# Attention, Fourier mixing and a feed-forward on one core: sums of four split over two engines, folds taken crosswise, special columns in two column groups

## The chip, the core and the metric

The kernel runs on one core of a Trainium2 chip. The core has TensorE (PE: matmuls, into the eight banks of PSUM), VectorE (DVE), ScalarE (ACT) and GpSimd (POOL) for elementwise work, and SyncE (SP), whose queue issues most DMAs here; GpSimd's queue issues the rest. Every engine works through its own queue in order and waits on semaphores for the others. The metric is the device time of one execution in microseconds, the median of several runs.

## What is computed

Eight batches of eight heads, 576 positions, head size 64. Attention is the sum of two parts: one over means of four neighbouring positions, repeated four times, and one over positions less than four apart. Its output goes through a two-dimensional Fourier transform, of which the real part is added, then a layer norm and a feed-forward with a width of 2048.

```python
q_d = q.reshape(B, H, Sd, factor, D).mean(axis=3)     # factor 4, Sd = 144; k_d, v_d alike
out_up = np.repeat(sm_attn(q_d, k_d, v_d), factor, axis=2)
mask = np.abs(pos[:, None] - pos[None, :]) < factor
...                                                   # softmax of the masked scores
x = out_up + out_local                                # as (B, S, H * D)
mixed = np.real(np.fft.fft(np.fft.fft(x, axis=1), axis=2))
u = x + mixed
un = (u - mu) / np.sqrt(var + 1e-06)
return u + np.maximum(un @ w_ch1, 0.0) @ w_ch2
```

## The kernel before

There are three kinds of work, and they overlap. `Unit` (40 of them, five for each batch) loads a span of 128 positions of queries and keys (`qkT`, six buffers) and of values (`vaug`), sums queries and keys in fours (`sum_in`, L603, into `sums`), computes the local attention of two windows of 64 positions and writes it to `xa` (front half of the positions) and `xb` (the back half, in reversed order). `Pooled` (one for each batch) computes the attention over the sums of four: `scores` (L473) need `sums` of all five units of the batch; `pool_v` (L447) sums the values by matmuls in groups of 32 array columns; the result goes to `odt`, and `pack` sends a last piece by DMA into slot 2 of `xa`.

`Mix` (one for each batch) is the Fourier transform, as matmuls with cosine and sine tables. Since cosine is even and sine odd, the work is halved by folding the positions (front with back) and the channels (1 to 255 with 511 to 257) before the matmuls. `half_sum` (L744, VectorE) and `half_difference` (L747, GpSimd) fold positions, 512 columns each for each of three slots, into `xs` and `xm` (`halves`); `channels` (L755, VectorE) folds channels, 255 columns with the second input reversed; `fold` (L768, VectorE for the sum and GpSimd for the difference) folds once more into `f`; `sequence` (L793) is the matmul over positions, `mix` (L832, L828) the one over channels, `unfold` (L851) undoes the folds, and the stores go to DRAM. Channels 0 and 256 have no partner. `split_z` (L781, ScalarE) copies them into `zs`, padded with zeros to 66 columns; `sequence_z` (L808) multiplies them, eight matmul passes for a batch (four slots, two passes each in float32); `z_high` and `z_low` (L811, L814) copy rows 0 to 3 of the result and its rounding rest to rows 0 to 3 and 32 to 35 of `yz`, which `clear_yz` has zeroed; `mix` adds them with the rows of `signs`.

`Quarter` decodes the weights (64 pieces; ScalarE, GpSimd, three VectorE operations, ScalarE, GpSimd). `Block` (nine, of 512 tokens) is norm and feed-forward: `first` (L1172) and `second` (L1192 to L1194) are its matmuls in the first three blocks; the later six use a product with fewer multiplications (L1110), for which `Differences` prepares differences of weights.

The order is written out by hand. `at(fn)` gives each call a place from `TURNS`, in the order of the calls of its kind; calls without a place come after all others, by a time `t` that the planner counts. All calls are then made in the order of places, and each engine's queue and each DMA queue is filled in that order. There are 1574 places: the attention, the mixing, the weights, block 0 and part of block 1 have them. No call can overtake another on its engine. PSUM banks are handed out in that order too.

Of the kernel before, what the change touches and what calls it, by code (L numbers as in the profile page):

```python
# [8 lines left out]
F32 = mybir.dt.float32  # L9
# [4 lines left out]
ALU = mybir.AluOpType  # L14
# [8 lines left out]
ZCOLS = 66  # L23
# [3 lines left out]
    "Pooled.pool_v": (49, 130, 261, 398, 518, 677, 799, 920),  # L27
    "Pooled.copy_v": (50, 132, 263, 399, 520, 680, 800, 925),
# [4 lines left out]
    "Pooled.maxima": (  # L33
        43, 19, 20, 166, 83, 109, 283, 207, 224, 427, 332, 353, 552, 488, 511, 697, 617, 641, 823, 746, 770,
        952, 865, 891,
    ),
    "Pooled.exps": (
        46, 23, 30, 173, 86, 115, 288, 216, 231, 435, 339, 361, 558, 502, 519, 703, 620, 650, 837, 756, 780,
        954, 869, 896,
    ),  # L40
    "Pooled.transpose_p": (
        59, 26, 35, 176, 110, 134, 312, 228, 265, 441, 351, 386, 584, 503, 523, 710, 643, 683, 839, 774, 806,
        958, 894, 926,
    ),
    "Pooled.copy_p": (
        68, 29, 56, 190, 114, 139, 315, 234, 268, 443, 360, 410, 588, 509, 533, 714, 649, 687, 846, 779, 816,
        964, 897, 931,
    ),
    "Pooled.values": (
        88, 51, 62, 198, 133, 142, 320, 264, 277, 445, 400, 413, 602, 522, 537, 727, 684, 698, 852, 803, 821,  # L50
        965, 927, 949,
    ),
    "Pooled.result": (
        93, 54, 71, 202, 155, 154, 323, 273, 284, 454, 408, 416, 605, 542, 544, 730, 694, 701, 856, 809, 826,
        972, 935, 951,
    ),
    "Pooled.store": (97, 212, 392, 463, 626, 750, 878, 975),
    "Pooled.pack": (100, 213, 342, 493, 624, 747, 871, 977),
    "Mix.half_sum": (
        120, 91, 125, 247, 252, 253, 352, 355, 372, 513, 515, 526, 636, 658, 662, 763, 762, 786, 887, 905, 904,  # L60
        1000, 1004, 1003,
    ),
    "Mix.half_difference": (
        112, 95, 111, 219, 255, 280, 356, 379, 380, 504, 529, 531, 646, 663, 665, 767, 795, 794, 885, 918, 915,
        999, 994, 1009,
    ),
    "Mix.channels": (
# [4 lines left out]
    ),  # L72
    "Mix.fold": (
# [4 lines left out]
    ),  # L78
    "Mix.split_z": (84, 137, 191, 287, 362, 382, 535, 534, 681, 686, 777, 836, 930, 921, 983, 1014),
    "Mix.sequence_z": (165, 311, 440, 573, 705, 841, 960, 1016),  # L80
    "Mix.z_high": (175, 316, 457, 587, 715, 847, 1022, 1054),
    "Mix.z_low": (182, 326, 474, 590, 720, 859, 1031, 1064),
    "Mix.sequence": (
        181, 180, 178, 179, 330, 331, 329, 327, 480, 481, 465, 466, 608, 615, 576, 586, 740, 743, 741, 739, 860,
        861, 879, 881, 1010, 1011, 987, 1007, 1071, 1070, 1107, 1102,
    ),
    "Mix.sequence_out": (193, 189, 341, 337, 484, 470, 621, 597, 755, 754, 868, 886, 1021, 1024, 1120, 1111),
    "Mix.mix": (
        239, 266, 227, 260, 350, 368, 385, 387, 366, 418, 497, 521, 500, 536, 642, 654, 631, 685, 676, 678, 772,
        804, 768, 773, 895, 900, 928, 957, 893, 901, 1069, 1072, 1068, 1029, 1131, 1157, 1186, 1214, 1185, 1213,  # L90
    ),
    "Mix.even_out": (
        262, 235, 363, 389, 390, 501, 508, 648, 634, 679, 778, 775, 898, 933, 922, 1079, 1080, 1143, 1208, 1194,
    ),
    "Mix.unfold": (
        281, 286, 270, 271, 375, 374, 404, 403, 425, 426, 539, 543, 549, 551, 660, 659, 702, 695, 689, 690, 814,
        813, 788, 787, 911, 910, 969, 968, 934, 939, 1098, 1134, 1101, 1099, 1178, 1180, 1233, 1232, 1217, 1219,
    ),
    "Mix.store_mixed": (307, 423, 625, 708, 876, 976, 1159, 1235),
    "Mix.store_local": (143, 150, 244, 309, 394, 462, 564, 572, 707, 668, 752, 783, 877, 973, 998, 1006),  # L100
    "Mix.store_ends": (496, 835, 974, 1220),
    "Unit.load": (
        2, 3, 1, 0, 7, 40, 41, 58, 57, 38, 99, 146, 147, 145, 148, 243, 149, 246, 208, 245, 396, 424, 421, 391,
        461, 568, 567, 569, 571, 595, 623, 669, 667, 709, 670, 785, 748, 832, 784, 833,
    ),
    "Unit.sum_in": (
        9, 10, 11, 12, 13, 42, 53, 64, 66, 73, 168, 172, 183, 184, 185, 282, 297, 300, 321, 324, 432, 449, 450,
        475, 477, 579, 583, 591, 593, 607, 688, 696, 733, 734, 735, 829, 830, 853, 855, 857,
    ),
    "Unit.load_v": (  # L110
        8, 36, 37, 39, 4, 5, 102, 98, 101, 103, 211, 242, 144, 209, 241, 308, 345, 393, 395, 346, 397, 490, 492,
        491, 494, 565, 627, 628, 596, 666, 751, 671, 753, 749, 782, 834, 874, 875, 872, 873,
    ),
    "Unit.scores": (
        14, 15, 25, 61, 48, 74, 104, 117, 119, 141, 199, 220, 236, 237, 319, 291, 365, 384, 420, 447, 468, 517,
        545, 585, 601, 610, 629, 652, 699, 725, 726, 781, 802, 820, 825, 864, 899, 943, 940, 956,
    ),
    "Unit.maxima": (
        21, 18, 45, 65, 52, 80, 107, 121, 123, 169, 206, 223, 275, 250, 333, 299, 373, 409, 429, 451, 478, 524,
        553, 592, 603, 618, 635, 656, 700, 731, 736, 790, 808, 824, 828, 866, 908, 953, 944, 967,  # L120
    ),
    "Unit.exps": (
        24, 22, 47, 70, 55, 85, 113, 131, 135, 174, 215, 230, 289, 259, 338, 303, 383, 434, 444, 458, 485, 532,
        559, 599, 619, 622, 647, 672, 704, 737, 738, 801, 815, 838, 844, 870, 923, 955, 948, 978,
    ),
    "Unit.transpose_p": (
        27, 28, 60, 75, 89, 116, 118, 164, 177, 204, 229, 238, 293, 294, 347, 367, 412, 446, 469, 499, 547, 546,
        577, 609, 632, 674, 653, 711, 712, 760, 759, 805, 840, 842, 880, 919, 929, 981, 959, 980,
    ),
    "Unit.copy_p": (  # L130
        31, 32, 67, 78, 94, 129, 138, 188, 195, 214, 233, 258, 304, 305, 358, 388, 436, 456, 472, 506, 557, 556,
        589, 611, 644, 682, 673, 716, 723, 764, 776, 817, 845, 849, 883, 924, 932, 982, 961, 990,
    ),
    "Unit.values": (
# [111 lines left out]
def kernel(  # L246
# [475 lines left out]
    for t in (zs, *(t[:, :, DM:] for t in halves)):  # L722
        nc.gpsimd.memset(t, 0.0)
# [729 lines left out]
```

## Time and profile before

| | us |
|---|---|
| median of 3 runs | 1124.72 |
| lowest and highest run | 1123.99, 1129.9 |
| span of the profiled execution (its first to its last instruction) | 1124.3 |
| TensorE busy in it | 1070.8 |
| VectorE, ScalarE, GpSimd busy | 637.6, 401.0, 352.0 |

The profile is one execution. Busy time is the union of an engine's instructions; matmul passes are pipelined, so many of them overlap, and the mean time of one pass is longer than its share of the busy time. A chain of waits is followed back from the last instruction: at each step to what released it, or to the instruction before it on its engine. "SPq" is time in SyncE's queue, "issue" time in which the engine waited for nothing that the profile shows.

### The profile page before, as it was taken

The numbers are of one execution on the slowest core, as the hardware profiler recorded it, in microseconds if no ns is written. First come the engines' busy times: TensorE is split into PE (matmuls) and PEld (weight loads), VectorE is DVE, ScalarE is ACT, GpSimd is POOL, SyncE is SP. The second block draws the span as 40 slices with busy tenths as digits, with TensorE's granted clock in tenths as the row PEclk, the third lists the DMA queues.
The fourth block names the chain that finished last, engine by engine and source line by source line (L and its number), as shares of the span: only waits on it lengthen the run. The fifth ranks groups of instructions, "written<-read, shape, count | busy, mean of one in ns | idle before, by whom it ended". The sixth has DMA issues, their size and how long they took to land.

```text
span 1124.3 us, 24306 instructions
## 1 busy us (share of the span) xinstructions
PE 1070.8 (95%) x9316; PEld 899.0 (80%) x9316; DVE 637.6 (57%) x1298; ACT 401.0 (36%) x1122; POOL 352.0 (31%) x501
## 2 busy tenths in 40 slices
PE   7787998999999999999999999999999999999998
PEld 5565766777778888887788889888989889889997
DVE  4778889988999885452314533443443343353333
ACT  4756565675444442132221231232232132132121
POOL 1313231233475553487331140331231331222000
PEclk9999999999999999999999999999999999999999
DMA  6545647676685444478709845955955975875641
GB/s 246 187 168 189 223 140 226 226 229 175 181 193 169 123 122 140 111 241 279 194 1 278 245 152 166 314 171 160 298 194 162 259 236 159 221 252 183 216 160 38
DMA packets 121451, 214.36 MB, mean 191 GB/s; under 512 B 14576, under 2 KB 30992, under 8 KB 121208
## 3 DMA queue, kind: packets, MB, share of 16 engines
q1 hardware_dynamic: 110056, 191.97, 52.0%
q0 software_dynamic: 11280, 20.84, 10.2%
q8 instruction: 74, 1.21, 0.4%
q14 instruction: 41, 0.34, 0.1%
HBM read 166.86 MB, written 45.42 MB: 189 GB/s over the span
## 4 chain that ended last, share of the span: by engine, by line
PE 67%; DMA 13%; DVE 9%; SPq 4%; POOL 3%; issue 3%; ACT 2%; DVEq 0%; ACTq 0%; POOLq 0%
PE banks L1110 18%; PE banks L1192 10%; PE banks L1193 10%; PE banks L1194 10%; PE banks L1172 7%; PE banks L793 3%; DMA w1l<-ut 2%; DMA qkT<-in_qk_dram 2%; DMA w1h<-ut 2%; PE banks L832 2%; PE banks L522 1%; DMA raw<-in_wq_dram 1%; DMA vaug<-in_vw_dram 1%; PE banks L1039 1%; DMA out_dram<-ut 1%
## 5 line engine op out<-in xcount | busy, mean ns | idle before, releaser
L1192 PE MATMUL banks<-w2h,hh 128*128 128x512 f32 x576 | 228.4, 397 | 0.7 <-ACT hh L1176 0.7
L1194 PE MATMUL banks<-w2h,hl 128*128 128x512 f32 x576 | 225.0, 391 | 0.8 <-DVE hl L1180 0.8
L1193 PE MATMUL banks<-w2l,hh 128*128 128x512 f32 x576 | 225.4, 391 | 0.0
L1176 ACT ACTIVATE hh<-row 128x512 fp32r<-128x512 f32 x96 | 60.6, 632 | 285.8 <-DVE row L1135 194.2
L1135 DVE TENSOR_TENSOR row<-wt,banks 128x256 f32<-128x256 f32 x192 | 80.4, 419 | 142.9 <-PE banks L1110 138.7
L1180 DVE SCALAR_TENSOR_TENSOR hl<-row,hh 128x512 fp32r<-128x512 f32 x96 | 68.9, 718 | 118.8 <-ACT hh L1176 118.8
L1194 PEld LDWEIGHTS banks<-w2h,hl 128*128 128x128 f32 x576 | 108.2, 188 | 25.5 <-DVE hl L1180 1.7
L1192 PEld LDWEIGHTS banks<-w2h,hh 128*128 128x128 f32 x576 | 108.5, 188 | 20.7 <-ACT hh L1176 1.1
L1193 PEld LDWEIGHTS banks<-w2l,hh 128*128 128x128 f32 x576 | 108.6, 188 | 19.2
L1172 PE MATMUL banks<-unT,w1h 128*128 128x512 f32 x384 | 102.3, 392 | 0.6 <-DVE unT L1048 0.6
L1172 PEld LDWEIGHTS banks<-unT,w1h 128*128 128x128 f32 x384 | 71.7, 188 | 16.4 <-DVE unT L1048 1.0
L1009 POOL DMA_DIRECT2D ut<-ux x40 | 35.7, 1034 | 152.4 <-DMA ut<-um 124.7
L1180 DVE SCALAR_TENSOR_TENSOR hl<-banks,hh 128x512 fp32r<-128x512 f32 x48 | 32.8, 688 | 77.5 <-ACT hh L1176 77.5
L639 ACT ACTIVATE sb<-banks,mx 128x64 f32<-128x64 f32 x320 | 70.0, 330 | 1.3
L1130 ACT COPY wt<-banks 128x256 f32<-128x256 f32 x96 | 35.8, 372 | 95.4 <-PE banks L1110 95.4
L793 PE MATMUL banks<-seq,f 128*128 128x290 f32 x256 | 67.0, 412 | 2.1 <-ACT sb L639 1.4
L1110 PE MATMUL banks<-w1h,w1h 128*128 128x256 f32 x384 | 62.0, 283 | 3.1 <-DMA w1h<-ut 3.0
L1110 PE MATMUL banks<-w1h,w1l 128*128 128x256 f32 x384 | 62.6, 285 | 2.4 <-DMA w1l<-ut 2.0
L1110 PE MATMUL banks<-unT,w1h 128*128 128x256 f32 x432 | 63.4, 283 | 0.0
L1110 PE MATMUL banks<-unT,w1l 128*128 128x256 f32 x432 | 63.2, 282 | 0.0
L1110 PEld LDWEIGHTS banks<-unT,w1h 128*128 128x128 f32 x432 | 59.8, 190 | 3.9
L1110 PEld LDWEIGHTS banks<-unT,w1l 128*128 128x128 f32 x432 | 59.8, 191 | 3.7
(122 smaller groups left out, 1929.1 us busy)
## 6 DMA issues: line engine op xcount, KB each, us to landing
w1l<-ut SPq DMA_DIRECT2D x96, 256.0 KB
w1h<-ut SPq DMA_DIRECT2D x96, 256.0 KB
qkT<-in_qk_dram SPq DMA_DIRECT2D x40, 512.0 KB
w1h<-ub SPq DMA_DIRECT2D x72, 256.0 KB
w1l<-ub SPq DMA_DIRECT2D x72, 256.0 KB
raw<-in_wq_dram SPq DMA_DIRECT2D x64, 256.0 KB
vaug<-in_vw_dram SPq DMA_DIRECT2D x40, 260.0 KB
out_dram<-ut SPq DMA_DIRECT2D x36, 256.0 KB
```

The costliest lines, as they stand in the source:

```text
L639: nc.scalar.activation(out=self.sb[:, hp, z], in_=self.sc[:, z, hp], func=AF.Exp, scale=0.125, bias=self.mx[:, z, hp : hp + 1],)
L793: nc.tensor.matmul(y, l, r, start=(i == 0), stop=(i == len(mms) - 1))
L1009: nc.gpsimd.dma_start(out=to, in_=ux[b][k0 : k0 + m, :], accum_op=ALU.add)
L1110: nc.tensor.matmul(into, w[:, y, c, :], both[z][:, c, :], start=(start and i == 0), stop=(i == len(mms) - 1), skip_group_check=True)
L1130: nc.scalar.copy(out=joins[k].bitcast(F32), in_=self.ps[x])
L1135: nc.vector.tensor_add(out=place(to), in0=place(a), in1=self.ps[x])
L1172: nc.tensor.matmul(hps, a[:, c, :], unT[:, x, c, :], start=(i == 0), stop=(i == len(mms) - 1))
L1176: nc.scalar.activation(out=hh, in_=self.hps[f], func=AF.Relu)
L1180: nc.vector.scalar_tensor_tensor(out=hl, in0=self.hps[f], scalar=0.0, in1=self.hh[f].bitcast(F32), op0=ALU.max, op1=ALU.subtract)
L1192: nc.tensor.matmul(acc, hh, w2h, start=start, stop=False)
L1193: nc.tensor.matmul(acc, hh, w2l, start=False, stop=False)
L1194: nc.tensor.matmul(acc, hl, w2h, start=False, stop=stop)
```

## The change

Three edits of the arithmetic, and new places for all calls.

Sums of four: `pair_in` adds elements 0, 1 to elements 2, 3 of each four on GpSimd (512 columns out, into `half`, two buffers), and `sum_in` adds the two halves on VectorE, in place of one reduction over four.

Crosswise folds: `cross` adds near channels 1 to 255 of one half of the positions to the reversed far channels of the other half, once each way (VectorE for the one, GpSimd for the other, 255 columns each). `channels` then takes sum and difference of the two. `half_sum` and `half_difference` go.

Special columns: `split_z` adds channels 0 and 256 of both halves on GpSimd (three slots) and copies those of the pooled part on ScalarE. `zs` has 32 columns. `sequence_z` sends slots alternately to output rows 0 to 31 and 32 to 63; `z_high` and `z_low` copy all 64 rows; `signs` has ones in each group of 32 and so adds the groups. `clear_yz` goes.

Places: 1937 calls have one now. New are those of the first three blocks to their end, of the start of block 3, and of `Differences`.

```diff
-ZCOLS = 66
+ZCOLS = 32
 TURNS = {
     "Pooled.scores": (
-        33, 17, 16, 163, 77, 105, 276, 200, 221, 419, 328, 348, 548, 483, 498, 675, 614, 633, 818, 744, 758,
-        950, 862, 882,
+        41, 34, 40, 160, 90, 105, 292, 228, 259, 420, 365, 390, 576, 508, 537, 713, 647, 652, 843, 789, 806,
+        962, 914, 924,
     ),
+    "Unit.pair_in": (
+        5, 1, 21, 24, 9, 38, 79, 67, 28, 50, 162, 192, 106, 202, 213, 346, 288, 335, 294, 352, 452, 472, 378,
+        483, 453, 598, 603, 627, 630, 619, 692, 775, 675, 738, 761, 783, 872, 780, 877, 888,
     ),
...
+        def pair_in(self):
+
+            self.half = pd.tile([P, 2 * HP, GU, 2], F32, name="half", bufs=2)
+            x = self.qkT.rearrange("p i h (g r) -> p (i h) g r", r=4)
+            nc.gpsimd.tensor_add(out=self.half, in0=x[:, :, :, 0:2], in1=x[:, :, :, 2:4])
+
         def sum_in(self):
...
-            x = self.qkT.rearrange("p i h (g r) -> p (i h) g r", r=4)
+            x = self.half
             n = sum(g < GH for g in groups_of(self.m))
             for a, e in ((0, n), (n, GU)):
                 if a < e:
                     to = out[:, :, a:e] if e == n else out[:, :, a:e][:, :, ::-1]
-                    nc.vector.tensor_reduce(out=to, in_=x[:, :, a:e], axis=AX.X, op=ALU.add)
+                    nc.vector.tensor_add(out=to, in0=x[:, :, a:e, 0], in1=x[:, :, a:e, 1])
...
-        def half_sum(self, t):
-            nc.vector.tensor_add(out=halves[0][:, t, :DM], in0=xa[:, t], in1=xb[:, t])
-
-        def half_difference(self, t):
-            nc.gpsimd.tensor_sub(out=halves[1][:, t, :DM], in0=xa[:, t], in1=xb[:, t])
+        def cross(self, t, back):
+            near, far = (xb, xa) if back else (xa, xb)
+            (nc.gpsimd if back else nc.vector).tensor_tensor(
+                out=crossed[back][:, t, 1:HD], in0=near[:, t, 1:HD], in1=far[:, t, DM - 1 : HD : -1], op=ALU.add
+            )
...
-            src = odt[:, 0] if t == NSL else halves[odd][:, t]
+            if t == NSL:
+                a, b = odt[:, 0, 1:HD], odt[:, 0, DM - 1 : HD : -1]
+            else:
+                a, b = (x[:, t, 1:HD] for x in crossed)
             nc.vector.tensor_tensor(
-                out=self.w[t][:, odd, 1:HD],
-                in0=src[:, 1:HD],
-                in1=src[:, DM - 1 : HD : -1],
-                op=ALU.subtract if odd else ALU.add,
+                out=self.w[t][:, odd, 1:HD], in0=a, in1=b, op=ALU.subtract if odd else ALU.add
             )
...
         def split_z(self, pooled):
+            cols = slice(0, HD + 1, HD)
             if pooled:
-                z, x = zs[:, NSL:], odt[:, 0:1, 0 : HD + 1 : HD]
+                nc.scalar.copy(out=zs[:, NSL:, 0:2], in_=odt[:, 0:1, cols])
             else:
-                z, x = zs[:, :NSL], halves[0][:, :, 0 : HD + 1 : HD]
-            nc.scalar.copy(out=z[:, :, 0:2], in_=x)
+                nc.gpsimd.tensor_add(out=zs[:, :NSL, 0:2], in0=xa[:, :, cols], in1=xb[:, :, cols])
...
         def sequence_z(self):
 
-            y = self.yzp = bank(self, "yz", ZCOLS)[:, 0, :KEPT]
-            mms = self.slots(zs, 0)
-            for i, (l, r) in enumerate(mms):
-                nc.tensor.matmul(y, l, r, start=(i == 0), stop=(i == len(mms) - 1))
+            y = self.yzp = bank(self, "yz", 2 * ZCOLS)[:, 0, :KEPT]
+            for i, (l, r) in enumerate(self.slots(zs, 0)):
+                g = i % 2 * ZCOLS
+                nc.tensor.matmul(y[g : g + ZCOLS], l, r, start=(i < 2), stop=(i >= 2), skip_group_check=True)
 
         def z_high(self):
-            nc.scalar.copy(out=yz[0:4, self.mine], in_=self.yzp[0:4])
+            nc.scalar.copy(out=yz[: 2 * ZCOLS, self.mine], in_=self.yzp)
 
         def z_low(self):
-            nc.vector.tensor_sub(out=yz[32:36, self.mine], in0=self.yzp[0:4], in1=yz[0:4, self.mine].bitcast(F32))
+            high = yz[: 2 * ZCOLS, self.mine].bitcast(F32)
+            nc.vector.tensor_sub(out=yz[2 * ZCOLS :, self.mine], in0=self.yzp, in1=high)
...
-    signs[[0, 2, 32, 34]] = 1.0
-    signs[[1, 3, 33, 35]] = [1.0, -1.0]
+    signs[0::32] = 1.0
+    signs[1::32] = [1.0, -1.0]
```

## Rows read from the trace of the kernel before

**Rows 1.** The page: busy us (share, instructions) of engines; busy tenths in 40 slices.
```profile
PE 1070.8 (95%) x9316; PEld 899.0 (80%) x9316; DVE 637.6 (57%) x1298; ACT 401.0 (36%) x1122; POOL 352.0 (31%) x501
...
PE   7787998999999999999999999999999999999998
...
DVE  4778889988999885452314533443443343353333
```

**Rows 2.** Three stretches: length, busy us by engine, granted clock, DMA share, GB/s.
```profile
0.00:336.00 336.00, 297.45 (x4930) 222.99 (x4931) 278.04 (x571) 191.17 (x661) 109.31 (x162) 0.98 0.65 199
336.00:588.00 252.00, 250.16 (x1118) 204.91 (x1117) 138.25 (x263) 80.24 (x189) 135.47 (x195) 1.00 0.53 154
588.00:1124.30 536.30, 523.18 (x3271) 471.12 (x3270) 221.31 (x465) 129.61 (x273) 107.27 (x144) 1.00 0.66 202
```

**Rows 3.** The chain of waits, 0 to 340 us: shares by line; start, us, what.
```profile
by line: PE banks L793 10.1%; DMA qkT<-in_qk_dram 6.6%; issue 5.7%; PE banks L522 4.4%; DMA raw<-in_wq_dram 4.4%; DMA vaug<-in_vw_dram 4.3%; PE banks L832 4.0%; DVE sums L603 3.1%; DMA um<-o 2.9%; PE banks L652 2.8%; SPq L884 2.8%; PE banks
...
9.83 4.67 DVE sums L603 x5
...
92.31 1.74 DVE xs L744 x2
```

**Rows 4.** Groups by line and shape: busy us, mean ns of one, idle before.
```profile
L603 DVE TENSOR_REDUCE sums<-qkT 128x256 f32<-128x1024 f32 x32 | 38.4, 1211 | 12.4 <-DMA qkT<-in_qk_dram 8.0 <-PE banks L473 4.3
L747 POOL TENSOR_TENSOR xm<-xa,xb 128x512 f32<-128x512 f32 x24 | 35.4, 1481 | 39.2 <-DMA xa<-rest 19.9 <-DVE xb L700 13.7 <-DMA vaug<-in_vw_dram 5.5
L768 POOL TENSOR_TENSOR f<-w 128x256 f32<-128x256 f32 x32 | 26.6, 845 | 62.0 <-DVE w L755 57.8 <-DVE rsd L534 4.3
L744 DVE TENSOR_TENSOR xs<-xa,xb 128x512 f32<-128x512 f32 x24 | 19.0, 805 | 5.8 <-DMA xa<-rest 5.6
L768 DVE TENSOR_TENSOR f<-w 128x256 f32<-128x256 f32 x32 | 18.1, 571 | 0.1
L808 PE MATMUL banks<-seq,z 128*66 128x290 f32 x64 | 17.1, 410 | 0.4 <-DVE ends L851 0.4
L447 PE MATMUL banks<-vaug,poolm 128*32 128x260 f32 x128 | 11.0, 414 | 5.5 <-DMA vaug<-in_vw_dram 5.3 <-ACT ptd L507 0.2
L603 DVE TENSOR_REDUCE sums<-qkT 128x136 f32<-128x544 f32 x8 | 5.7, 711 | 0.0
L603 DVE TENSOR_REDUCE sums<-qkT 128x120 f32<-128x480 f32 x8 | 5.2, 646 | 0.1
```

**Rows 5.** VectorE in order of time, 87.5 to 100: start, us, line, what.
```profile
87.86 0.69 DVE L744 TENSOR_TENSOR xs<-xa,xb 128x512 f32<-128x512 f32 x1 [2.31 <-DMA xa<-rest]
88.58 1.37 DVE L755 TENSOR_TENSOR w<-xs 128x255 f32<-128x255 f32 x1
...
97.47 0.41 DVE L755 TENSOR_TENSOR w<-xs 128x255 f32<-128x255 f32 x1
...
99.00 1.21 DVE L603 TENSOR_REDUCE sums<-qkT 128x256 f32<-128x1024 f32 x1
```

**Rows 6.** GpSimd in order of time, the same stretch.
```profile
87.99 3.11 POOL L747 TENSOR_TENSOR xm<-xa,xb 128x512 f32<-128x512 f32 x2 [3.69 <-DMA xa<-rest]
...
99.02 1.30 POOL L747 TENSOR_TENSOR xm<-xa,xb 128x512 f32<-128x512 f32 x1
```

**Rows 7.** TensorE in order of time, from 247.8 us.
```profile
247.84 2.12 PE L808 MATMUL banks<-seq,z 128*66 128x290 f32 x8
249.80 0.60 PE L652 MATMUL banks<-ident,sb 128*128 128x128 f32 x4
```

**Rows 8.** TensorE in order of time, from 284.8 us.
```profile
284.77 2.12 PE L808 MATMUL banks<-seq,z 128*66 128x290 f32 x8
286.82 0.73 PE L522 MATMUL banks<-vsum,ptd 128*32 128x65 f32 x32
```

**Rows 9.** Who waited for whom, 0 to 340, TensorE: us, times, longest.
```profile
PE banks L473 <- DVE sums L603: 3.8, 2, 3.6
```

**Rows 10.** Who waited for whom, 0 to 340, GpSimd.
```profile
POOL f L768 <- DVE w L755: 57.8, 14, 10.1
```

More of the change, by code (lines that the diff above doesn't have):

```diff
@@ L66 @@
+        1005, 966, 979,
+    ),
+    "Pooled.store": (
+        97, 234, 344, 513, 674, 765, 958, 989,
+    ),
+    "Pooled.pack": (
+        132, 199, 366, 518, 651, 784, 904, 1016,
+    ),
+    "Mix.cross": (
[3 rows of a table added]
     ),
     "Mix.channels": (
[4 rows of a table removed]
[4 rows of a table added]
     ),
     "Mix.fold": (
[4 rows of a table removed]
-    ),
-    "Mix.split_z": (84, 137, 191, 287, 362, 382, 535, 534, 681, 686, 777, 836, 930, 921, 983, 1014),
-    "Mix.sequence_z": (165, 311, 440, 573, 705, 841, 960, 1016),
-    "Mix.z_high": (175, 316, 457, 587, 715, 847, 1022, 1054),
@@ L82 @@
-    "Mix.z_low": (182, 326, 474, 590, 720, 859, 1031, 1064),
[4 rows of a table added]
+    ),
+    "Mix.split_z": (
+        109, 143, 226, 284, 400, 413, 464, 581, 702, 688, 746, 830, 893, 969, 1025, 1029,
+    ),
+    "Mix.sequence_z": (
+        150, 313, 462, 586, 728, 857, 999, 1046,
+    ),
+    "Mix.z_high": (
+        157, 326, 465, 588, 739, 884, 1022, 1076,
+    ),
+    "Mix.z_low": (
+        165, 328, 482, 591, 752, 889, 1035, 1093,
+    ),
     "Mix.sequence": (
-        181, 180, 178, 179, 330, 331, 329, 327, 480, 481, 465, 466, 608, 615, 576, 586, 740, 743, 741, 739, 860,
-        861, 879, 881, 1010, 1011, 987, 1007, 1071, 1070, 1107, 1102,
-    ),
@@ L148 @@
+        604, 617, 628, 662, 680, 764, 741, 791, 798, 805, 867, 912, 902, 930, 935, 977, 991, 1017, 1013,
+        1028,
+    ),
+    "constants": (
+        46,
+    ),
+    "close_b": (
+        1034,
+    ),
+    "close_a": (
+        1054,
+    ),
+    "close_e": (
+        1161,
+    ),
+    "close_d": (
+        1341,
+    ),
     "Block.load": (
-        570, 798, 912, 566, 765, 884, 563, 796, 917, 344, 612, 916, 1042, 1077, 1087, 1034, 1060, 1085, 1043,
-        1095, 1135, 1040, 1117, 1148, 1553, 1561, 1566, 1555, 1562, 1570, 1556, 1563, 1572, 1557, 1565, 1573,
-    ),
@@ L171 @@
[L171 to L174 removed]
[3 rows of a table added]
+    ),
+    "Block.finish": (
+        1276, 1283, 1345, 1356, 1463, 1415, 1455, 1412, 1626, 1609, 1602, 1618, 1761, 1741, 1747, 1748, 1927,
+        1928, 1921, 1922,
+    ),
+    "Block.store": (
+        1632, 1621, 1613, 1627, 1814, 1765, 1757, 1756, 1934, 1935, 1924, 1930,
+    ),
+    "Block.turn_copy": (
+        1905, 1886, 1881, 1892,
+    ),
@@ new lines @@
+    "Block.add_up": (
+        1919, 1896,
+    ),
+    "Block.sum_high": (
+        1925, 1901, 1931, 1899, 1929, 1912, 1923, 1897,
+    ),
+    "Block.sum_low": (
+        1932, 1911, 1936, 1904, 1933, 1916, 1926, 1902,
+    ),
+    "Differences.rejoin": (
+        1585, 1610, 1655, 1694, 1722, 1775, 1803, 1845,
+    ),
+    "Differences.differ": (
+        1587, 1615, 1657, 1704, 1738, 1779, 1809, 1847,
+    ),
+    "Differences.high": (
+        1590, 1595, 1588, 1598, 1617, 1620, 1628, 1619, 1668, 1661, 1672, 1659, 1714, 1718, 1708, 1715, 1746,
+        1742, 1753, 1752, 1780, 1783, 1791, 1788, 1821, 1810, 1811, 1818, 1848, 1855, 1852, 1850,
+    ),
@@ L708, in plan @@
             for fn in (
-                *(self.load, self.sum_in, self.load_v, self.scores, self.maxima, self.exps),
+                *(self.load, self.pair_in, self.sum_in, self.load_v, self.scores, self.maxima, self.exps),
                 *(self.transpose_p, self.copy_p, self.values, self.result),
@@ L888, in plan @@
             for slot in reversed(range(NSL)):
-                at(self.half_sum, slot)
-                at(self.half_difference, slot)
+                for back in range(2):
+                    at(self.cross, slot, back)
             for slot in reversed(range(NSL + 1)):
@@ L1234 @@
     at(constants)
-    at(clear_yz)
     def close_b():
```

162 lines of the change are left out of this document (85 added, 77 removed), and 86 rows, old and new, of the table TURNS.

## The prediction

> **What bounds the kernel now.** I read the busy shares first, then three stretches of the span, then the chain of the first stretch, then the groups that the change touches.
>
> TensorE is busy for 1070.8 of the 1124.3 us, and its line of tenths is below 9 almost only in the first quarter [rows 1]. The stretches put numbers on it: of 0 to 336 us (attention and Fourier mixing) TensorE works 297.5, so it idles 38.5; of the 252 us behind, 1.8; of the last 536 us, 13.1 [rows 2]. So whatever shortens the first stretch, or takes work off TensorE anywhere, shortens the whole, and idle time of the other engines after 336 us buys nothing. In the first stretch VectorE is nearly as full as TensorE: 278 of 336 us, its line at 7 to 9, with GpSimd at a third (109 us) [rows 1, 2]. The chain through it is mixed: matmuls, landings of query and key tiles, and the reduction of `sum_in` (L603) with 3.1% of 340 us, which is 10.5 us [rows 3]. Landings, SP's issues and matmuls that the change leaves alone make up most of the rest.
>
> The profiled execution spans 1124.3 us; the median of the runs is 1124.72, so 0.4 us lie around the span. I take the sum off 1124.3 and keep the 0.4.
>
> **The sums of four.** Removed: 48 VectorE reductions (40 units, eight of them in two pieces), 38.4 + 5.7 + 5.2 = 49.3 us [rows 4]. Added on VectorE: 48 adds with a quarter as many elements in each input. The nearest row is an add of 255 columns with both inputs in SBUF, 0.41 us undisturbed [rows 5]; 32 x 0.42, and for the 16 half-size pieces 0.27 (the line through 255 columns at 0.41 and 512 at 0.69 [rows 5], taken to 128), give 17.8 us: minus 31. Added on GpSimd: 40 pairwise adds of 512 elements. The 512-column GpSimd row costs 1.48 us mean [rows 4] and 1.30 undisturbed [rows 6]; its operands are contiguous, the new ones go in pairs of two with a stride of four. I take 1.48, so 59 us; below 1.30 nothing speaks for it, and above I allow double (2.96) for the stride, which would be 118 us and belongs to the slower rival. At 59 us they cost nothing by themselves, because GpSimd is idle for 227 of the 336 us [rows 2].
>
> On the chain, 10.5 us of reductions become 10.5 x 0.42/1.21 = 3.7: minus 6.8. But the add now stands behind the GpSimd add, so where a reduction on the chain follows a landing, 1.5 us come in. I see that at the start (five reductions in a row, 4.67 us [rows 3]), and assume one more such place: plus 3. The pooled scores must wait for two engines instead of one, and what is queued behind a late pair add is everything else on GpSimd: folds, crosswise adds, the weights' clamps and low parts. The loads' buffers, six of them, are now given back by GpSimd rather than VectorE.
>
> **The crosswise folds.** Removed: 24 VectorE adds of 512 columns (19.0 us) and 24 GpSimd subtractions (35.4 us). Added: 24 + 24 adds of 255 columns, one input reversed. The present channel adds have just that form, 0.41 us undisturbed [rows 5], and GpSimd's reversed fold of 256 columns is 0.85 us [rows 4]. So VectorE: 24 x (0.685 - 0.412) = minus 6.5 undisturbed (0.69 is the row at 87.86 us [rows 5]); GpSimd: 24 x (1.48 - 0.85) = minus 15. Six of the old adds are on the chain, about 0.75 each [rows 3], 4.5 us; to 0.42 each that is minus 2. The channel adds behind keep their size and only change operands: nothing.
>
> **The special columns.** The 64 matmul passes of `sequence_z` (eight for each of eight batches) take 17.1 us [rows 4], 2.12 us for a batch's eight, from start to the next matmul 1.96 [rows 7]. They get 32 columns instead of 66 and alternate between two column groups. That groups of 32 run at once shows in `pool_v`: 128 passes over 260 columns in 11.0 us, 86 ns each, against 267 for the passes here [rows 4]. Two groups give four steps of 0.244 us ((2.12 - 0.41)/7, one pass being 0.41 [rows 4, 7]) in place of eight, if passes pair freely, five if they pair only between neighbours. Against that stand two changes of the array's form: the same eight passes took 2.05 us when a differently shaped matmul followed [rows 8] and 1.96 when none did, so 0.09 each. Per batch 1.96 becomes 1.16 to 1.40: minus 6.4 to minus 4.5 for all eight; I take 6 off TensorE's work, and with its share of idle time there 5.3 off the path. Clearing `yz` (one ScalarE pass) goes, `split_z` moves eight copies of six columns from ScalarE to GpSimd (below 0.85 us each, the 256-column row; off the path, but in GpSimd's queue they wait for the last attention result, and the pair adds behind them too), and the two copies of `yz` keep 290 columns on more partitions: nothing, covered by ScalarE's 191 busy us of 336 [rows 2].
>
> **Disturbance.** The row at 88.58 shows an add with two SBUF inputs taking 1.37 us instead of 0.41 while GpSimd works from 87.99 to 91.10 [rows 5, 6]; the reduction at 99.00 stays at 1.21 beside a GpSimd subtraction from 99.02 [rows 5, 6]. So the change swaps the form that isn't disturbed for one that is, and gives the disturber more work. Now the excess is 18.1 - 32 x 0.415 = 4.8 us for VectorE's folds and 19.0 - 24 x 0.685 = 2.6 for the old sums [rows 4], together 7.4 over 56 adds, 0.13 each. GpSimd goes from 109 to 109 + 59 - 15 = 153 us, times 1.4; 168 adds (48 + 24 + 64 + 32) instead of 120 give 168 x 0.13 x 1.4 - 120 x 0.13 = plus 15 us on VectorE. What is left of its relief: 31 + 6.5 - 15 = 22 us of 278, or 8%.
>
> The Trainium skill says so more strictly ("SBUF — State Buffer", "Who interferes with whom"): a VectorE reduction never contends with GpSimd, one with two SBUF inputs does, and the second to issue fully blocks. Both rows agree with it. By it each new add that meets a GpSimd add would wait for its end, which is the third rival below.
>
> **Places set anew.** All places change, those of DMA issues too: loads, stores, weight fetches on SP's queue, and the accumulating loads on GpSimd's, behind which pair adds now stand. The new list also fixes the order of the first three blocks and the weight differences to their end, where the old one stopped earlier. No row prices this. It can't gain more than the idle time: 38.5 us in the first stretch, 1.8 in the second. As a loss I bound it with the slower rival. I take minus 2, for an eased VectorE that ends PE waits sooner: it released TensorE directly in waits such as 3.8 us for the sums [rows 9].
>
> **Sum.** -6.8 + 3 - 2 - 5.3 - 2 = -13: 1124.3 - 13 + 0.4, about 1111 us.
>
> **Rivals.**
> 1. The first stretch fills up. With VectorE eased, TensorE idles there nearly as little as behind: its line shows 9 there, so at most a tenth [rows 1], and the last 536 us have 2.4% [rows 2]. I take 4%; 336 x 0.04 = 13 instead of 38.5, and 6 off its work: minus 31, less some start-up that can't go: 1097. For it: VectorE is the other full engine. Against it: the chain has much DMA that is unchanged.
> 2. Column groups don't overlap. Then TensorE keeps 17.1 us and pays 16 x 0.09 = 1.4: 1111 + 5.3 + 1.4 = 1118. `pool_v` speaks against it.
> 3. Lost to the shared port. If each of 48 pair sums waits out one GpSimd add, VectorE gets 48 x 1.3 = 62 us and loses its 37: plus 25, of which I let a third reach the path, 8, the chain being mixed; TensorE's 5.3 and the 2 for the order stay: about plus 1, 1126, no change. For it: the row of 1.37 us. Against: today's VectorE folds lose 4.8/32 = 0.15 us each, not 1.3.
> 4. Slower: GpSimd's queue takes VectorE's place ahead of the pooled scores. GpSimd has waited for VectorE in 14 places before its folds, 57.8 us, 4.1 each [rows 10]. A pair add behind such a fold holds up the sums, and TensorE stands at the scores in its fixed order. In the third batch the last pair add has place 213, the scores 228; 336 us hold some 1240 places, so 15 are 4.1 us, of which both adds need 1.9. The slack of 2.2 is less than one such wait. Each batch hit costs about 4.1; three of eight eat the gain of 13; six give 25 - 13 = plus 12: about 1137.
>
> **How the numbers follow.** Forecast (1104 to 1118): 0.42; rival 1: 0.22; rival 2: 0.06; rival 3: 0.15; rival 4: 0.15. About 0.5%, 5.6 us, is what a measurement of this kernel can tell from no change. Rival 2 lies on that border and is split 0.04 to 0.02. Faster 0.42 + 0.22 + 0.04 = 0.68, same 0.17, slower 0.15. For 8 in 10 the range leaves out the lower quarter of rival 1 (below 1092) and most of rival 4 (above 1131).
>
> **What would show it.** Right: `sequence_z` at about 9 to 11 us with passes of the two groups starting together; VectorE in the first stretch some 20 to 25 us less busy; GpSimd at about 150 us with pair adds near 1.4; TensorE idle below 30 us in the first stretch and the last 536 us unchanged. Wrong: pair adds far above 1.5 us; long waits of TensorE's pooled scores for `sums`; folds and pair sums near 0.9 us mean (rival 3); or idle time of TensorE appearing between 336 and 588 us, where the new list also sets the order.

## Result: 1.5% faster

| | median, us | ratio to before, 95% interval |
|---|---|---|
| before, first measurement | 1127.31 | 1 |
| after, first measurement | 1113.35 | 0.9885 (0.9846 to 0.9924) |
| before, measured again | 1126.41 | 1 |
| after, measured again | 1110.34 | 0.9852 (0.9827 to 0.9876) |
| predicted | 1111, range 1092 to 1131 | |

The sum came out where it should, and so did the sign; several of the terms inside it did not. Here is first what the trace of after shows.

The page, as [rows 1]: busy us of the engines, then the tenths of two of them.

```profile
PE 1059.4 (96%) x9316; PEld 886.3 (80%) x9316; DVE 605.3 (55%) x1298; ACT 399.1 (36%) x1113; POOL 374.1 (34%) x547
...
PE   7999999999899999799999999999999999999998
...
DVE  4898878778887873343333533533444443353333
```

TensorE's line stands at 9 from the second slice on, where before it stood at 7 to 9 for a quarter of the span, and it has two new dents, one at the eleventh slice and one at the seventeenth. The three stretches of [rows 2]:

```profile
0.00:336.00 336.00, 310.81 (x5059) 230.86 (x5060) 267.00 (x626) 203.86 (x684) 149.91 (x232) 0.99 0.69 213
336.00:588.00 252.00, 240.22 (x1085) 197.71 (x1085) 124.38 (x223) 68.80 (x163) 117.16 (x172) 0.98 0.51 150
588.00:1109.10 521.10, 508.35 (x3175) 457.72 (x3173) 213.91 (x451) 126.48 (x266) 107.01 (x144) 1.00 0.66 202
```

TensorE idles 25.2 us in the first (38.5 before), 11.8 in the second (1.8 before), 12.8 in the third (13.1). So time was won in the attention and part of it given back in the 252 us behind. The second trace of the changed kernel shows the same, 9.8 us idle there, so this is no chance of one profile:

```profile
336.00:588.00 252.00, 242.22 (x1088) 199.83 (x1087) 122.75 (x219) 68.78 (x163) 116.73 (x172) 0.97 0.52 151
```

The span shrank by 15.2 us in the first trace: 11.4 of them are less busy time of TensorE (7.7 from the special columns), 3.8 less idle time. In the second trace it shrank by 19.2, 6.8 busy and 12.4 idle. One trace alone doesn't fix this split.

A finer cut, by stage, of before and then of after:

```profile
0.00:250.00 250.00, 215.50 (x3963) 160.25 (x3964) 199.82 (x406) 149.77 (x537) 64.24 (x98) 0.98 0.63 206
250.00:420.00 170.00, 165.94 (x1344) 131.59 (x1343) 150.60 (x316) 79.67 (x221) 89.86 (x140) 1.00 0.58 160
420.00:588.00 168.00, 166.16 (x743) 136.06 (x742) 65.86 (x113) 41.96 (x95) 90.69 (x120) 1.00 0.55 162
```

```profile
0.00:250.00 250.00, 232.88 (x4624) 170.96 (x4626) 196.75 (x473) 170.90 (x604) 106.35 (x161) 0.99 0.71 227
250.00:420.00 170.00, 157.18 (x774) 123.92 (x771) 130.81 (x272) 64.62 (x163) 86.23 (x141) 0.99 0.53 155
420.00:588.00 168.00, 160.97 (x749) 133.69 (x748) 63.83 (x104) 37.15 (x83) 74.49 (x102) 0.98 0.55 156
```

Idle TensorE: 34.5 to 17.1 us in the first 250, minus 17.4; 4.1 to 12.8 and 1.8 to 7.0 behind, plus 13.9. The same in landmarks, the matmuls of the local attention's values and of the first feed-forward layer of the slow blocks (min/median/max ns, first and last start), of before and then of after:

```profile
L680 PE MATMUL banks<-vaug,pT x1280: 217/218/368, 23.9 to 292.3; 64*64 64x65 f32 x183
...
L1172 PE MATMUL banks<-unT,w1h x384: 387/389/607, 313.9 to 587.4; 128*128 128x512 f32 x192
```

```profile
L779 PE MATMUL banks<-vaug,pT x1280: 213/218/268, 20.7 to 255.9; 64*64 64x65 f32 x183
...
L1268 PE MATMUL banks<-unT,w1h x384: 387/389/793, 280.6 to 571.5; 128*128 128x512 f32 x192
```

The attention ends 36 us earlier, the feed-forward starts 33 us earlier, the first three (slow) blocks end 16 us earlier, and that is about what the whole gains. Their feed-forward takes 291 us instead of 273, from its first to its last start.

The groups that the change touches, as [rows 4]; L690 is `pair_in`, L702 `sum_in`, L840 `cross`, L863 `fold`, L903 `sequence_z`:

```profile
L690 POOL TENSOR_TENSOR half<-qkT 128x512 f32<-128x512 f32 x40 | 42.5, 1067 | 44.1 <-DVE sums L702 18.6 <-DMA qkT<-in_qk_dram 11.4 <-DVE rs L796 6.3
...
L840 POOL TENSOR_TENSOR xq<-xb,xa 128x255 f32<-128x255 f32 x24 | 18.8, 787 | 21.6 <-DVE xb L799 13.9 <-DMA xa<-rest 7.7
L863 DVE TENSOR_TENSOR f<-w 128x256 f32<-128x256 f32 x32 | 16.1, 512 | 0.1
L702 DVE TENSOR_TENSOR sums<-half 128x256 f32<-128x256 f32 x32 | 14.7, 473 | 8.9 <-POOL half L690 6.1 <-PE banks L566 2.6
L840 DVE TENSOR_TENSOR xp<-xa,xb 128x255 f32<-128x255 f32 x24 | 14.0, 592 | 0.0
...
L903 PE MATMUL banks<-seq,z 128*32 128x290 f32 x64 | 9.4, 413 | 0.0
...
L702 DVE TENSOR_TENSOR sums<-half 128x120 f32<-128x120 f32 x8 | 3.6, 447 | 0.0
...
L702 DVE TENSOR_TENSOR sums<-half 128x136 f32<-128x136 f32 x8 | 2.4, 294 | 0.0
```

The sums cost VectorE 20.7 us instead of 49.3, the cross folds 14.0 instead of 19.0. The special columns take 9.4 us instead of 17.1: eight passes in 1.17 us here, which took 2.12 in [rows 7]. The passes of the two groups start in pairs, 6 to 10 ns apart, so there are four steps where there were eight.

```profile
43.76 1.17 PE L903 MATMUL banks<-seq,z 128*32 128x290 f32 x8
44.86 0.55 PE L751 MATMUL banks<-ident,sb 128*128 128x128 f32 x3
```

### The profile page after: what moved, and what is told of

Its sections match the earlier page's. It is cut to its first block, busy times and chain, and to the rows that moved or that the text cites. A ratio compares the mean times of both kernels' runs of the same rounds, so it can differ in the third digit from the quotient of the medians.

```text
span 1109.1 us, 24327 instructions
## 1 busy us (share of the span) xinstructions
PE 1059.4 (96%) x9316; PEld 886.3 (80%) x9316; DVE 605.3 (55%) x1298; ACT 399.1 (36%) x1113; POOL 374.1 (34%) x547
## 3 DMA queue, kind: packets, MB, share of 16 engines
q8 instruction: 74, 1.21, 0.5%
## 4 chain that ended last, share of the span: by engine, by line
PE 65%; DMA 14%; DVE 8%; issue 5%; POOL 3%; SPq 2%; ACT 2%; DVEq 0%; ACTq 0%; POOLq 0%
PE banks L1206 19%; PE banks L1288 9%; PE banks L1289 9%; PE banks L1290 9%; PE banks L1268 5%; DMA w1l<-ut 4%; PE banks L888 3%; DMA raw<-in_wq_dram 3%; DMA ux<-xa 1%; DMA vaug<-in_vw_dram 1%; PE banks L615 1%; PE banks L1135 1%; PE banks L928 1%; DVE wt L450 1%; PE banks L779 1%
## 5 line engine op out<-in xcount | busy, mean ns | idle before, releaser
L1268 PEld LDWEIGHTS banks<-unT,w1h 128*128 128x128 f32 x384 | 73.1, 191 | 25.2 <-DVE hl L1276 6.3
L1120 POOL TENSOR_TENSOR rstd<-rstd,mhalf 128x1 f32<-128x1 f32 x36 | 20.5, 568 | 148.7 <-DVE rstd L1119 148.7
```

Of the source, the lines that this page charges most:

```text
L1268: nc.tensor.matmul(hps, a[:, c, :], unT[:, x, c, :], start=(i == 0), stop=(i == len(mms) - 1))
```

## Experiments

Two theories stood against each other at first. A: the arithmetic gives the gain (VectorE's relief, and TensorE's shorter special columns), the new places little. B: the new places give it. All ratios are to the kernel before, measured beside each variant; 0.001 is 1.1 us. A difference of two ratios, and so each cost below, is uncertain by about 4 us.

### The arithmetic in the old places

```diff
+    "Mix.cross": places of half_sum and half_difference, in turn
+    "Unit.pair_in": place of sum_in - 0.5
```

> The changed arithmetic in the places of before: each pair sum stands directly ahead of its sum, the crosswise adds in the places of half sum and half difference (four of 48 moved just ahead of their channel folds). Theory A: 8 to 12 us below before, 0.989 to 0.993, nearly all of the gain; VectorE about 20 us less busy in the first 336 us, TensorE 7 us less work. Theory B: within 5 us of before, above 0.995. If pair sums one place ahead of the sums make TensorE wait for the pooled scores, slower than before by 5 us or more.

Measured: 1.0111 (1.0087 to 1.0136), 13 us slower than before and 29 slower than the changed kernel. Both theories miss, and the time is the one expected for a wait of the pooled scores: the arithmetic alone loses time. Its waits for the pair sums, VectorE's and GpSimd's own, from 0 to 340 us:

```profile
DVE sums L485 <- POOL half L473: 32.0, 14, 8.7
```

```profile
POOL half L473 <- DMA qkT<-in_qk_dram: 35.1, 9, 9.5
```

In the changed kernel the same two waits are

```profile
DVE sums L702 <- POOL half L690: 6.1, 2, 5.1
```

```profile
POOL half L690 <- DMA qkT<-in_qk_dram: 11.4, 8, 3.0
```

VectorE's work fell to 162.9 us in the first 250 (199.8 before), and TensorE's fell with it, from 215.5 to 206.5: a relieved engine that stands and waits.

```profile
0.00:250.00 250.00, 206.45 (x3790) 152.19 (x3791) 162.93 (x391) 141.99 (x502) 87.61 (x134) 0.95 0.60 196
```

GpSimd's queue does take VectorE's place, as my fourth rival has it, but not where that rival looks for the loss: TensorE's own wait at the pooled scores grew only from 3.8 us [rows 9] to 6.0, while its idle time up to 588 us grew from 40.4 to 56.0.

```profile
PE banks L349 <- DVE sums L485: 6.0, 2, 4.2
```

### The new places with the old arithmetic

```diff
-        pair_in, cross, two groups of 32 columns
+        sum_in as one reduction, half_sum and half_difference, one group of 66
```

> The new places with the arithmetic of before: reductions on VectorE, half sums and differences of 512 columns in the places of the crosswise adds, special columns in one group of 66; the copy of special columns is moved behind the last half sum in five batches. Theory A: at before or slower, 0.995 to 1.01, attention ending 30 us later than in the changed kernel. Theory B: 0.985 to 0.992.

Measured: 1.0065 (1.0041 to 1.0088). So B falls too, and A's half about the places is confirmed in its sign: the new places alone cost 7 us. The attention ends 21 us later than in the changed kernel, at 276.5 us, where 30 were expected. In the new places, the arithmetic is worth 0.0213, 24 us.

### One part undone at a time, in the new places

The sums of four back on VectorE alone:

```diff
-        pair_in: nc.gpsimd.tensor_add(out=self.half, in0=x[:, :, :, 0:2], in1=x[:, :, :, 2:4])
-                    nc.vector.tensor_add(out=to, in0=x[:, :, a:e, 0], in1=x[:, :, a:e, 1])
+                    nc.vector.tensor_reduce(out=to, in_=x[:, :, a:e], axis=AX.X, op=ALU.add)
```

> The changed kernel with one part undone: queries and keys are summed in fours by one VectorE reduction in the place of the second sum, the GpSimd pair sum is left out; result unchanged. Theory A: 6 to 9 us slower than the changed kernel (0.993 to 0.997 of before), VectorE 25 us busier in the first 336 us, attention ending 7 us or more later. Theory B: within 3 us of the changed kernel. If the shared port had eaten the relief (third rival), the same or faster than the changed kernel.

The special columns back in one group of 66:

```diff
-                nc.tensor.matmul(y[g : g + ZCOLS], l, r, start=(i < 2), stop=(i >= 2), skip_group_check=True)
+                nc.tensor.matmul(y, l, r, start=(i == 0), stop=(i == len(mms) - 1))
```

> The changed kernel with one part undone: the special columns go through one group of 66 columns, with the clearing of their buffer. Theory C (TensorE's work counts nearly in full, since it is the fuller engine): 5 to 8 us slower than the changed kernel, 0.990 to 0.993 of before, the matmuls back at 17 us. Rival: they lie in idle time of TensorE that is there anyway; within 2 us of the changed kernel, 0.985 to 0.987.

The position folds back to 512 columns:

```diff
-        cross(t, 0), cross(t, 1): 255 columns each
+        half_sum(t) on VectorE, half_difference(t) on GpSimd: 512 columns each, in the places of cross
```

> The changed kernel with one part undone: half sums (VectorE) and half differences (GpSimd) of 512 columns in the places of the crosswise adds; special columns and pair sums as changed. The term of my sum: 2 us slower than the changed kernel. Since undoing the pair sums cost 13 us where I had 4, the same scale gives 4 to 8: 0.989 to 0.992 of before. Rival: the folds are covered by other work; within 2 us.

The changed kernel itself was measured beside the sums of four only; the other two are compared with it through the kernel before:

> The changed kernel once more, beside the variants below and with more rounds. Theory A (VectorE's relief and TensorE's shorter special columns give the gain, the new places little): 0.985 to 0.992 of before, as seen. Theory B (the new places give the gain) expects the same here. A chance effect of one profile would show as a stretch 336 to 588 us without the 11.8 us of idle TensorE.

| undone | ratio, 95% interval | costs, against 0.9852 |
|---|---|---|
| nothing | 0.9852 (0.9827 to 0.9876) | |
| sums of four | 0.9965 (0.9943 to 0.9987) | 13 us |
| position folds | 0.9936 (0.9913 to 0.9958) | 9 us |
| special columns | 0.9892 (0.9867 to 0.9917) | 4.5 us |

The costs add up to 27 us, which agrees with the 24 of all three within the intervals. The sums of four count for more than theory A's 6 to 9 us; without them the attention ends at 271.8 us instead of 255.9. The special columns count for 4.5 of the 7.7 us of matmul time that they give up, between theory C and its rival; with 4 us of uncertainty that doesn't show whether part of the time was idle anyway. The folds count for more than the 5 us that VectorE saves on them from before to after. In the kernel with the folds undone, VectorE's half sums read

```profile
L840 DVE TENSOR_TENSOR xs<-xa,xb 128x512 f32<-128x512 f32 x24 | 26.8, 1121 | 1.6 <-DMA xa<-rest 1.6
```

1.12 us each, where they took 0.81 before [rows 4] and 0.69 undisturbed [rows 5]. Without pair sums, in the same new places (the old arithmetic above), they read

```profile
L630 DVE TENSOR_TENSOR xs<-xa,xb 128x512 f32<-128x512 f32 x24 | 21.6, 905 | 0.0
```

So each half sum takes 0.10 us more in the new places and 0.22 more again with pair sums on GpSimd, and beside these the crosswise folds save VectorE 26.8 - 14.0 = 13 us, not 5. In the whole time this is not shown: without pair sums (1.0065 against 0.9965) folds and special columns together give 11 us, beside them 9 + 4.5, which is the same within the intervals.

### Does the distance of the pair sums from the sums matter?

First in the new places, with each pair sum directly ahead of its sum:

```diff
-    "Unit.pair_in": as changed, in the median 14 places ahead of sum_in
+    "Unit.pair_in": place of sum_in - 0.5
```

> The changed kernel with its places, but each pair sum directly ahead of its sum instead of 14 places in the median. If the distance matters (VectorE waits for GpSimd, and GpSimd's queue is short of slack): 5 to 15 us slower than the changed kernel, 0.990 to 0.999 of before, with VectorE waiting 20 us or more for pair sums in the first 340 us against 6. If the order of loads and all else carries it: within 3 us of the changed kernel.

Measured: 0.9951 (0.9931 to 0.9970), 11 us slower than the changed kernel. The time came as expected, the wait only in part:

```profile
DVE sums L495 <- POOL half L483: 11.6, 4, 5.4
```

So the distance counts, but what it costs is spread over more than VectorE's wait for the pair sums. The attention ends at 265.9 us, 10 later than in the changed kernel; TensorE has idled 41 us by 588 us, against 37 and 30 in the two traces of the changed kernel.

Then in the old places, with the pair sums earlier and more buffers:

```diff
-    "Unit.pair_in": place of sum_in - 0.5;  name="half", bufs=2
+    "Unit.pair_in": up to 14 places ahead of sum_in, behind the load;  name="half", bufs=4
```

> The changed arithmetic in the old places again, but with the pair sums up to 14 places ahead of their sums (the median distance in the new places) and four buffers for them. Theory D (the old places lost because VectorE stood before the pair sums, 32 us in 14 waits): that wait falls below 10 us and the time to 0.985 to 0.995 of before. Rival E (the old places lose for another reason, the order of everything else being made for the old durations): still above 1.0, with VectorE's wait for the pair sums gone all the same.

Measured: 1.0082 (1.0052 to 1.0112), not clearly better than 1.0111. VectorE's wait is halved, GpSimd's has grown:

```profile
DVE sums L485 <- POOL half L473: 15.5, 5, 9.2
```

```profile
POOL half L473 <- DMA qkT<-in_qk_dram: 52.2, 12, 9.1
```

An earlier pair sum finds its tile not yet there more often (52 us of waits, 35 with the late ones), and what is behind it in GpSimd's queue stands with it. The time stays where rival E put it, but VectorE's wait is neither below 10 us nor gone, so the run doesn't decide between D and E. It shows that distance and buffers, as far as they could be had here, don't mend the old places.

Last, the old places without pair sums, but with crosswise folds and grouped columns:

```diff
-        pair_in and two-step sum_in
+        sum_in as one reduction
```

> The old places, with crosswise adds and grouped special columns, but the sums of four as one VectorE reduction as before. Theory H (in the old places the pair sums stand in GpSimd's queue waiting for landings, 35 to 52 us, and hold up folds and crosswise adds behind them): faster than before by 4 to 9 us, 0.992 to 0.997, attention ending before 292 us. Rival I (the old order suits none of the new parts, since the loads issue late): 1.005 or more, attention ending at 300 us or later.

Measured: 0.9995 (0.9972 to 1.0017), between the two expectations; the attention ends at 288.6 us, as theory H has it. Taking the pair sums away mends 13 us of the old places' loss. That removes GpSimd's stand at the landings and VectorE's wait for the pair sums at once, so it doesn't show which of them cost the time. The folds and special columns, worth 9 and 4.5 us in the new places, are worth nothing in the old ones. The reading that fits, though no run isolates it: in a fixed order, time that one engine saves goes into the next wait unless the calls behind it are moved up too.

### Where the gain is given back

In the trace of after TensorE waits 5.9 us near 462 us, the dent in the seventeenth slice. TensorE, VectorE and GpSimd around it, in order of time (start, us, line, what, idle before and who ended it):

```profile
456.36 1.07 PE L1268 MATMUL banks<-unT,w1h 128*128 128x512 f32 x4
...
467.86 2.07 PE L1268 MATMUL banks<-unT,w1h 128*128 128x512 f32 x4 [5.90 <-DVE hl L1276]
```

```profile
459.32 0.69 DVE L1116 BATCH_NORM_STATS2 st<-ut 128x6 f32<-128x512 f32 x1 [7.11 <-DMA ut<-ud]
...
463.32 3.89 DVE L1127 TENSOR_SCALAR un<-ut,mv,rstd 128x512 f32<-128x512 f32 x1 [0.66 <-POOL rstd L1120]
467.13 1.27 DVE L1276 SCALAR_TENSOR_TENSOR hl<-banks,hh 128x512 fp32r<-128x512 f32 x2
```

```profile
463.84 1.05 POOL L1066 TENSOR_TENSOR raw<-raw 128x256 fp32r<-128x256 f32 x1
464.53 1.71 POOL L1066 TENSOR_TENSOR wt<-wt 128x256 fp32r<-128x256 f32 x2
465.89 1.02 POOL L1066 TENSOR_TENSOR raw<-raw 128x256 fp32r<-128x256 f32 x1
```

The low part `hl`, on which TensorE waits, has its last input at 462.4 us (`hh`, from ScalarE). It stands in VectorE's queue behind the statistics of two tiles of block 2, which waited 7.1 us for a DMA, and a norm that takes 3.9 us instead of 0.55 beside GpSimd's subtractions. TensorE, which did nothing from 462.0 to 467.9 us, then has a granted clock of 0.58 for 4 us, most of it at the lower of its two levels (1.2 GHz); it was 1.00 before the stop and is 1.00 again from 472 us. Four matmuls like those that took 1.07 us at 456.36 take 2.07 here.

```profile
467.80:472.00 4.20, 4.14 (x11) 3.35 (x12) 1.80 (x4) 0.00 (x0) 0.00 (x0) 0.58 0.66 225
```

Four calls were moved behind that low part:

```diff
 "Block.stats", "Block.norm", tiles 1 and 2 of block 2
-        1670, 1675 and 1676, 1678
+        1681.1, 1681.2 and 1681.3, 1681.4          # "Block.low" of the wait: 1681
```

> The changed kernel with four calls moved: statistics and norm of two tiles of block 2 stand behind one more of the feed-forward's low parts on VectorE. If TensorE's wait of 5 to 6 us near 460 us comes from that low part standing behind a statistics that waits for a DMA and a norm that waits beside GpSimd: 3 to 6 us faster than the changed kernel, 0.980 to 0.983 of before. If the norm is late for the transposes then, or the same time is lost a few us on: within 2 us of it.

Measured: 0.9807 (0.9777 to 0.9836), a median of 1103.74 us, 5 us faster than the changed kernel, as expected (the difference, 0.0045, is barely larger than its uncertainty of 0.0038), and the fastest of all that compute the reference. The norm still takes 3.96 us in this trace, but TensorE's wait of 5.9 us is gone.

The other dent lies where weights are decoded for the first feed-forward blocks. Leaving the decode's VectorE part out of this kernel, and out of the kernel before:

```diff
         def join(self):
-            ...                         # three VectorE operations of 128 x 256
+            pass
```

> The changed kernel with the late norm, and the three VectorE operations of each of the 64 weight pieces left out (the weights, and so the output, are not the reference's). Theory F (what the attention gained is given back where VectorE decodes weights beside the first feed-forward blocks): TensorE's idle time between 250 and 420 us falls from about 11 to below 4 us, the slow blocks take 274 to 277 us from their first to their last matmul instead of 284, and the time falls by 8 to 14 us, to 0.969 to 0.974 of before. Rival G (the new list of places itself spreads those blocks, whatever VectorE does): less than 4 us, the blocks still at 282 or more.

> The kernel before with the same three operations of each weight piece left out (output not the reference's). TensorE idles there only 4 us from 250 to 400, so theory F expects at most 4 us less, 0.996 to 1.0. If the decode holds up the old kernel as much, 0.985 to 0.992.

Measured: 0.9688 (0.9666 to 0.9710) and 0.9960 (0.9940 to 0.9981). So the decode costs the late-norm kernel 0.0119, 13 us, and the kernel before 4.5 us. The two profiled executions of the late-norm kernels differ by only 6.3 us (1099.1 and 1092.8), the medians of all by 11.6; the traces below show about half of the gain. The stages of 250 to 420 and 420 to 588 us, with the decode:

```profile
250.00:420.00 170.00, 158.93 (x775) 125.83 (x772) 130.16 (x271) 64.67 (x159) 87.30 (x142) 0.98 0.53 155
420.00:588.00 168.00, 166.28 (x791) 138.65 (x790) 65.78 (x107) 37.82 (x83) 77.17 (x105) 1.00 0.59 173
```

and without:

```profile
250.00:420.00 170.00, 165.27 (x847) 131.86 (x846) 64.05 (x122) 66.43 (x177) 86.21 (x147) 0.98 0.56 163
420.00:588.00 168.00, 166.88 (x807) 139.97 (x806) 62.70 (x105) 38.16 (x85) 77.17 (x104) 1.00 0.61 174
```

TensorE's idle time in the first of them falls from 11.1 to 4.7 us, VectorE's work from 130 to 64; in the second it was mended already by the late norm (1.7, where after had 7.0). The first expectation asked for less than 4 us, so the size of this one is a little short, though the time is not. The matmuls of the first layer in the slow blocks, late norm with decode, the same without, and the kernel before without:

```profile
L1061 PE MATMUL banks<-unT,w1h x384: 387/389/610, 279.8 to 563.5; 128*128 128x512 f32 x192
```

```profile
L1050 PE MATMUL banks<-unT,w1h x384: 387/389/615, 286.1 to 557.1; 128*128 128x512 f32 x192
```

```profile
L1161 PE MATMUL banks<-unT,w1h x384: 387/389/610, 312.4 to 583.3; 128*128 128x512 f32 x192
```

Without the decode the slow blocks take 271 us in the new places as in the old (274 to 277 were expected), so rival G, by which the new list itself spreads them, is out, and theory F holds. But TensorE hardly stands there for want of decoded weights. What it waits for most between 250 and 420 us, with the decode, is again a low part in VectorE's queue, 4.9 us of the 11.1, and without the decode this falls to 1.7 us:

```profile
PE banks L1083 <- DVE hl L1069: 4.9, 3, 2.1
```

In the changed kernel the decode's last VectorE operation starts 20 us earlier than before (412.9 us, 432.8 before), while the feed-forward starts 33 us earlier. That fits more of its low parts standing behind the decode; no run moves the one against the other.

## Why the prediction was right, step by step

**The total** was right, and partly by luck: two large errors in the terms cancel. For the arithmetic I had 6.8 - 3 + 2 + 5.3 = 11 us of gain, and in the new places it gives 24; for the places I had 2 us of gain, and alone they lose 7.

**Sums of four.** VectorE's side was right: 31 us undisturbed forecast, 28.6 measured. GpSimd's price was too high, 1.48 forecast and 1.07 measured, below the 1.30 that I gave as the lower end; no cost of stride or pairs is seen. What they give on the path was mis-sized by far: I took 6.8 - 3 = 3.8 us, and undoing them costs 13. The step that failed is "on the chain": I credited only the 10.5 us for which reductions lay on the chain of before. VectorE was busy for 200 of the first 250 us, and what fits the 13 us is that every call behind a reduction came sooner too; no run shows this by itself.

**Position folds.** Forecast 2 us, measured 9. The same error, and a second one: the price of the old folds was taken from the kernel before (0.69 undisturbed, 0.75 on its chain), not beside pair sums (1.12).

**Special columns.** Forecast 9 to 11 us of matmul, 6 off the work and 5.3 off the path; measured 9.4, 7.7 and 4.5. Two groups do run at once in four steps. To the next matmul they take 1.10 us [the rows at 43.76], 0.12 more than four steps of 0.244, where I had 0.18 for the two changes of the array's form. This term was right in its mechanism; its 4.5 us is uncertain by about 4.

**Disturbance.** Forecast plus 15 us on VectorE. Folds, crosswise adds and sums of four lose (16.1 - 32 x 0.415) + (14.0 - 24 x 0.412) + (20.7 - 17.8) = 9.8 us, and the 64 channel adds 3.8: 13.7 us over 168 adds, 0.08 each where I had 0.18. By the same count the 120 adds of before lose 12.4, so the change adds 1 us and not 15. GpSimd is busy for 374 us in all, 22 more and not the 44 that I had, since its new adds are short. VectorE is busy for 32 us less, 605.3 against 637.6; I had 22. The rule of the Trainium skill ("SBUF — State Buffer", "Who interferes with whom"), by which a VectorE add with two SBUF inputs contends with GpSimd's reads and a reduction doesn't, still agrees with the rows: half sums of 1.12 us beside pair sums and 0.91 without, and reductions that keep their 1.21. What I got wrong is how often they would meet. The order moves it, since with the late pair sums the 168 adds lose 19.7 us instead of 13.7; but in the old places they lose 14.5, so disturbance isn't what made the old places slow.

**Places.** Forecast minus 2, with "no row prices this". Measured alone they are plus 7, and the arithmetic alone plus 13, but together minus 17. The sum treated places and arithmetic as terms that add, and they don't: here the form of the step failed, not only its size.

**The rivals.** The fourth, GpSimd's queue ahead of the pooled scores, forecast a loss that came in the old places (1.0111), and with the pair sums late 11 us of the gain go in the new ones; but TensorE's wait at the scores is 6.0 us there and 1.7 with the late pair sums, so its step from the queue to the scores isn't shown. In the changed kernel that wait is 0.3 us. The first, a first stretch that fills up, came half true: idle time fell to 25.2 us in 336, where it had 13, and part of the gain was lost behind. The second is out (9.4 us of special columns), and so is the third (0.08 us lost per add).

**What would show it.** Of the signs for it, the special columns (9.4 us), TensorE's idle time in the first stretch (25.2, below 30) and in the last (12.8 against 13.1) came. GpSimd's 150 us there came too (149.9), but by luck: its pair adds took 1.07 and not 1.4, and later work moved into the stretch, 41 us more there and 22 in all. VectorE's 20 to 25 us less did not come, 11 there and 32 in all. Of the signs against it, I named idle time between 336 and 588 us. It came: 10 us more there than before.

Open is how the loss of the old places divides between GpSimd's stand at the landings, VectorE's wait for the pair sums and the order of loads, stores and folds as a whole. That the folds and special columns give nothing there is measured, but not what takes their time. Open too is what in the new places matters: the order of the attention and the more than 300 later calls that have a place for the first time were always changed together.

## What to carry to other kernels

In a kernel with one fixed order on every engine, an edit and its order are one change: price the pair, since the edit in the old order can lose what the two together gain. A saving on a nearly full second engine can be worth more than the instructions that happen to lie on the chain of one profile: here 28.6 us less work on an engine that was 80% busy was worth 13, where the chain gave 4. And when an early stage gets shorter, look at once for the work that the next stage now runs beside; here weight decoding and one norm, both queued on VectorE ahead of low parts, took back 14 us of idle time.

## What the runs showed of the hardware

A GpSimd add of 512 elements that reads pairs with a stride of four from one tile took 1.03 us at best and 1.04 in the median. The subtractions of the same size on contiguous rows of two tiles, in the kernel before, took 1.26 at best and 1.36 in the median; why is not shown.

```profile
L690 POOL TENSOR_TENSOR half<-qkT x40: 1028/1038/1222, 5.0 to 219.3; 128x512 f32<-128x512 f32 x40
```

```profile
L747 POOL TENSOR_TENSOR xm<-xa,xb x24: 1260/1364/2227, 40.7 to 296.0; 128x512 f32<-128x512 f32 x24
```

A norm on VectorE (one SBUF tile and two per-partition scalars in, 512 columns) took 3.9 us instead of 0.54 where four GpSimd subtractions in a row ran beside it, and ended 0.3 us after the last of them:

```profile
L1127 DVE TENSOR_SCALAR un<-ut,mv,rstd x36: 534/541/3890, 259.3 to 985.2; 128x512 f32<-128x512 f32 x36
```

The longest of the 36 norms took 3.9 to 4.0 us in all nine traces with the new places, and at most 0.96 in the five with the old ones. This fits the norm waiting for GpSimd, and for several of its operations in a row; no run takes the subtractions away.
